# Rewriting the first attention of a gated two-branch layer, forward and backward, as two sweeps over head pairs

## The chip, the cores and the metric

The kernel runs on one core of one Trainium2 chip. The metric is the device time of one execution in microseconds; three runs of the kernel before gave a median of 16272.24 us (16250.68 to 16278.3). The engines are named as in the profile: PE is TensorE (matmuls; PEld its weight loads), DVE is VectorE, ACT is ScalarE, POOL is GpSimd, and SP and POOL are the queues that issue DMAs here.

## What is computed

The layer mixes two attentions of the same input with a gate, and the kernel returns the output and the gradients of eleven inputs (`grad_out` is given). All arrays are bf16.

```python
x = A_x                                            # (1, 2048, 576)
g = sigmoid((x * gate_w).sum(-1, keepdims=True))
out = g * A(x) + (1 - g) * B(x)

def A(x):                                          # 32 heads of 18, one shared K and V
    q = (x @ wq).reshape(1, 2048, 32, 18).transpose(0, 2, 1, 3)
    k, v = x @ wk, x @ wv                          # (1, 2048, 18)
    p = softmax(einsum('bhqd,bkd->bhqk', q, k) * 18 ** -0.5)
    o = einsum('bhqk,bkd->bhqd', p, v)
    return o.transpose(0, 2, 1, 3).reshape(1, 2048, 576) @ wo

def B(x):                                          # 64 segments of 32 tokens, 8 memory tokens
    mem = mem0
    for s in range(64):
        h = concatenate([mem, x[:, 32*s:32*s+32]])
        o = causal_attention(h, Wq, Wk, Wv) @ Wo   # 32 heads of 128
        mem, out_s = o[:, :8], o[:, 8:]
```

For the first attention the backward pass needs, per head, the probabilities P again, dP = dO V^T, dS = P (dP - delta) with delta the row sum of P dP, and from these dV = P^T dO, dK = dS^T Q and dQ = dS K.

## The kernel before

`build_full` calls the stages one after the other; a Tile framework draws the dependencies, orders the instructions of each engine ahead of time from a model of their costs, and places the waits. A tile with `bufs=n` has n buffers; one that is allocated again waits until the old contents have been used. [...]

Setup: `build_xT` (L161) transposes x, `load_A_weights` (L786) spreads the heads' 18 columns to 32, four heads to 128 columns, and `a_setup` (L813) makes K and V replicated on the four 32-row groups with a row of ones (`kaug`, `vaugT`), Q with a row that holds minus a bound of the scores (`qaugT`), and Q by token.

Forward sweep, `a_forward_attn` (L907): for each of 8 groups of four heads and 4 blocks of 512 queries, 16 iterations over 128 keys. Eight matmuls (L927; four row tiles of the array, each in two pieces of 256 columns) give the scores of four heads, two exponentials of 1024 columns (L932) the numerators, twelve matmuls in column tiles (L938; pieces of 171) the products with V and ones, and DVE adds them to an accumulator in SBUF (L940). At a block's end a matmul spreads the denominators and DVE inverts and normalizes. `a_forward_out` (L951) projects.

B follows: `b_forward` (L235), `make_transposed_weights` (L206), then `gate_combine_pass` (L655), which computes the gate, B's output projection from the stored oT, the output, dz, and the products da = g grad_out and db = (1-g) grad_out with db's transpose; `b_backward` (L414) and `b_epilogue` (L555).

Backward sweep, `a_backward` (L976): for each group of four heads it makes dO scaled by the denominators with a row for delta (`doaug`) and its form by token (`dotok`); then for each of 4 blocks of 512 keys and 16 tiles of 128 queries, one iteration: the scores again (L1067), four exponentials of 512 (L1072), dP (L1077), four products on DVE (L1082), dK by twelve matmuls (L1087) added to an SBUF accumulator by DVE (L1090), sixteen transposes of dS (L1095) and their copy to SBUF (L1097), dV (L1101, L1103), and dQ by sixteen matmuls and an addition (L1108, L1110). The four score tiles and the four dP tiles of an iteration share four PSUM banks (`b_sdA`). `a_final` (L1147) makes dx, dwq, dwk, dwv and dwo per tile of 128 tokens and adds the weight gradients in SBUF on DVE.

All matmuls go through `mm` (L97), transposes often through `tr` (L101), so L98 and L103 stand for many places; `evac` (L87) copies out of PSUM and alternates DVE (L93) and ACT (L95) by a counter. `pieces` (L42) cuts a matmul so that rows x columns x depth stay under 960000.

## Time and profile before

The profiled execution spans 16242.6 us, 29.6 us less than the median of the runs. Stages, cut by the first and last instruction of each (us from the span's start):

| stage | from, to | us |
|---|---|---|
| setup | 0, 167 | 167 |
| forward sweep of the first attention | 167, 1274 | 1107 |
| its output projection, B's weights loaded | 1274, 1388 | 114 |
| B forward | 1388, 6612 | 5224 |
| B's weights transposed | 6612, 6711 | 99 |
| gate and combine | 6711, 7075 | 364 |
| loads, B backward | 7075, 10122 | 3047 |
| B's weight gradients | 10122, 10985 | 863 |
| loads, transposes for the backward sweep | 10985, 11049 | 64 |
| backward sweep of the first attention | 11049, 15926 | 4877 |
| final pass | 15926, 16243 | 317 |

PE is busy 89% of the span, DVE 37%, ACT 26%, POOL 8%. A row of the groups gives line, engine, operation, out <- in, shapes and count, then busy us and mean ns of one, then the engine's idle time before them and what ended it. A shape K*M before the matmul's operand says how many rows and columns of the 128 x 128 array it uses. PEclk is the share of the full TensorE clock that was granted; a matmul's recorded time holds its latency too, so matmuls that follow each other overlap in the records. The timeline merges like instructions: start, length, engine, line, count.

### The profile page before, as it was taken

The page shows a single profiled execution, that of the slowest core. Times are in us where ns is not written, and L with a number is a line of the kernel's source. Part 1 is how long each engine was busy: PE and PEld are TensorE (multiplying, and loading weights), DVE is VectorE, ACT ScalarE, POOL GpSimd, SP SyncE. Part 2 cuts the span into 40 slices and gives each one's busy share as a digit, 9 for nine tenths or more (in the row PEclk, how much of TensorE's full clock was granted, in tenths as well). Part 3 has the DMA queues.
Part 4 walks back from the last instruction along what each step waited for, and adds up shares of the span by engine and source line. Part 5 has one row for each costly group of instructions (what it writes and reads, how often), then busy time and mean ns, then how long its engine had stood idle before and what let it go on. Part 6 is the DMA issues. An engine that isn't in the chain of part 4 may idle for free. (4 is left out here: it accounts for less than half of the span.)

```text
span 16242.6 us, 424152 instructions
## 1 busy us (share of the span) xinstructions
PE 14387.9 (89%) x194891; PEld 8837.7 (54%) x195001; DVE 6081.6 (37%) x8905; ACT 4154.2 (26%) x6200; POOL 1271.0 (8%) x2288
## 2 busy tenths in 40 slices
PE   8997999999999999769999999977898898898897
PEld 3334666666666666558888887333333333333333
DVE  3442333333333333323333333004454454454457
ACT  6882111111111111112222222002333333333330
POOL 0000000000000000111111111241000000000001
PEclk6555555555555555677777777995555555555556
DMA  1002111111111111442222223431000000000001
GB/s 44 9 9 97 37 39 39 39 39 39 39 39 39 38 38 39 144 138 83 85 80 82 83 85 97 135 105 47 13 1 13 13 1 13 13 1 13 7 1 50
DMA packets 473535, 780.13 MB, mean 48 GB/s; under 512 B 223841, under 2 KB 316818, under 8 KB 468866
## 3 DMA queue, kind: packets, MB, share of 16 engines
q1 hardware_dynamic: 357506, 429.32, 8.3%
q0 software_dynamic: 114240, 323.67, 5.8%
q8 instruction: 1524, 24.97, 0.6%
q14 instruction: 265, 2.17, 0.0%
HBM read 407.54 MB, written 345.18 MB: 46 GB/s over the span
## 5 line engine op out<-in xcount | busy, mean ns | idle before, releaser
L98 PEld LDWEIGHTS <-hTs 128*64 128x64 bf16 (+1 forms) x38400 | 1854.8, 150 | 951.9 <-DVE hTs L250 64.9
L1072 ACT ACTIVATE b_pexp<-b_sdA 128x512 bf16<-128x512 f32 x2048 | 1059.3, 609 | 1704.1 <-PE b_dkvp L98 1698.7
L1082 DVE TENSOR_TENSOR b_dsn<-b_sdA,b_pexp 128x512 bf16<-128x512 f32 x2048 | 1296.0, 684 | 290.9 <-PE b_sdA L98 288.9
L103 PE MATMUL b_ptrs<-identB,b_dsn 128*128 128x128 bf16 x8192 | 1245.8, 308 | 0.0
L98 PE MATMUL b_sdA<-b_kaug,b_qaug 19*128 19x256 bf16 x4096 | 1161.7, 401 | 5.4 <-ACT b_dotok L95 5.4
L98 PE MATMUL b_sdA<-b_vaugT,b_doaug 19*128 19x256 bf16 x4096 | 923.2, 395 | 179.2 <-ACT b_pexp L1072 178.3
L309 DVE RECIPROCAL rden<-pbank 64x512 f32<-64x512 f32 x256 | 840.5, 3322 | 482.6 <-PE pbank L98 482.6
L932 ACT ACTIVATE a_pexp<-a_sps 128x1024 bf16<-128x1024 f32 x1024 | 951.9, 1080 | 135.6 <-PE a_sps L98 128.9
L1090 DVE TENSOR_TENSOR b_dKTp<-b_dKTp,b_dkvp 128x512 f32<-128x512 f32 x512 | 351.8, 687 | 1563.7 <-PE b_dkvp L98 1563.7
L98 PE MATMUL pbank<-Wv,hTs 128*64 128x103 bf16 (+3 forms) x12800 | 912.4, 290 | 0.0
L103 PEld LDWEIGHTS <-b_dsn 128*128 128x128 bf16 x8192 | 705.5, 131 | 374.9 <-issue 374.9
L95 ACT COPY b_dsT<-b_ptrs 128x2048 bf16<-128x2048 bf16 x256 | 477.4, 1865 | 1458.5 <-PE b_ptrs L103 1458.5
L98 PE MATMUL b_dkvp<-b_dsn,b_qtokp 128*32 128x171 bf16 (+1 forms) x6144 | 813.7, 335 | 0.0
L98 PE MATMUL pbank<-Wq,hTs 128*64 128x103 bf16 (+1 forms) x10240 | 710.8, 290 | 85.7 <-DVE hTs L250 64.8
L98 PE MATMUL pbank<-Wqk,hTs 64*64 64x102 bf16 (+1 forms) x5120 | 752.8, 291 | 0.0
L98 PEld LDWEIGHTS <-b_qtokp 128*32 128x32 bf16 x6144 | 295.1, 110 | 786.2 <-issue 786.2
L98 PE MATMUL pbank<-Wk,hTs 128*64 128x103 bf16 (+1 forms) x10240 | 711.0, 290 | 0.0
L98 PE MATMUL pbank<-WoT,gTs 128*64 128x103 bf16 (+3 forms) x12800 | 644.6, 227 | 51.6 <-DMA WoT<-st_WoT 51.3
L98 PEld LDWEIGHTS <-b_doaug 19*128 19x128 bf16 x4096 | 220.5, 101 | 704.6 <-issue 704.4
L98 PE MATMUL a_sps<-a_qaugT,a_kaug 19*128 19x256 bf16 x4096 | 585.3, 402 | 1.1 <-ACT a_qtokp L95 1.1
L98 PEld LDWEIGHTS <-gTs 128*64 128x64 bf16 (+1 forms) x12800 | 458.8, 113 | 232.0 <-issue 52.4
L940 DVE TENSOR_TENSOR a_oacc<-a_oacc,a_pv 128x512 f32<-128x512 f32 x512 | 350.9, 685 | 565.0 <-PE a_pv L98 565.0
(409 smaller groups left out, 19900.9 us busy)
## 6 DMA issues: line engine op xcount, KB each, us to landing
st_q<-q SPq DMA_DIRECT2D x64, 512.0 KB
st_k<-k POOLq DMA_DIRECT2D x64, 512.0 KB, 3.0
st_vT<-vT SPq DMA_DIRECT2D x64, 512.0 KB
st_pnT<-pnT SPq DMA_DIRECT2D x64, 512.0 KB
st_oT<-oT POOLq DMA_DIRECT2D x64, 512.0 KB, 4.1
bq<-st_q SPq DMA_DIRECT2D x64, 512.0 KB
bvT<-st_vT SPq DMA_DIRECT2D x64, 512.0 KB
bk<-st_k POOLq DMA_DIRECT2D x64, 512.0 KB, 4.3
```

The lines of the kernel that those rows point to most:

```text
L95: nc.scalar.copy(out, in_)
L98: return self.nc.tensor.matmul(out, lhsT, rhs, start=start, stop=stop, tile_position=tp, skip_group_check=True)
L103: return self.nc.tensor.transpose(out, in_, self.identB[b:b + nrows, b:b + nrows], tile_position=tp)
L309: nc.vector.reciprocal(rden[rows, :], den[rows, :])
L932: nc.scalar.activation(pexp[:], spss[pr][:], ACT.Exp, scale=SCALEA)
L940: nc.vector.tensor_tensor(out=oacc[:, :], in0=oacc[:, :], in1=pv[:, :], op=ALU.add)
L1072: nc.scalar.activation(pe[:, :], sN[i][:, :], ACT.Exp, scale=SCALEA)
L1082: nc.vector.tensor_tensor(out=d_[:, :], in0=dps[i][:, :], in1=pexp[i][:, :], op=ALU.mult)
L1090: nc.vector.tensor_tensor(out=dKTp[:, k0:k0 + 512], in0=dKTp[:, k0:k0 + 512], in1=dkvp[:, :], op=ALU.add)
```

## The change

The first attention is rewritten around pairs of heads; each pair fills the four row groups of the array: two heads' Q and two heads' dO (rows 0, 32, 64, 96), against K, K, V, V.

- `prep` replaces `build_xT` and the gate's part of the combine pass: it loads x and grad_out whole, computes the gate, transposes x, da and db, and stores them. `combine_pass` keeps B's output projection, the output and dz; its pdg sums stay in PSUM.
- `a_weights`, `a_setup`: K and V in one tile `KV` (128 x 2048), and per key tile the stationary operands `VK` (V, a one, K) and `WK` (a one and K for the dP sums).
- `a_qd`: per pair and block of 512 queries, Q and dO in one tile `QD`, two column tiles at a time, with the score bound on Q; stored for the second sweep.
- `a_pass1` replaces the forward sweep. Per key tile: scores S of two heads, dP of two heads, E = exp(S), W = dP E, and four matmuls that add VK^T E and WK^T W into one PSUM bank over all 16 key tiles: sums of E, E V, E K, W and W K. `a_post` turns them at the block's end into O, delta and dQ = scale (WK - delta EK) / l, by token, mostly on POOL, and stores the scaled Q and dO (`SD`).
- `a_pass2` replaces the backward sweep's dK and dV. Delta has been put into two rows of the stored QD, so that dP comes out as dP - delta. Per block of 512 keys, over all 16 pairs and 16 query tiles: S, dP, E, dS = dP E, and four matmuls into one bank (dK of two heads, dV of two heads), copied out once per block.
- `a_out` projects O; `a_final` works on whole tensors kept in SBUF and adds the weight gradients in PSUM.

Matmuls of the first attention are no longer cut by `pieces`. The order of the stages is now prep, a_weights, a_setup, a_pass1, a_pass2, a_out, B forward, transposed weights, combine_pass, B backward, epilogue, a_final. The calls of `evac` without a named engine ahead of B forward go from 104 to 133, and the combine pass has none left (one per tile before).

The core of the diff (removed: `a_forward_attn` and `a_backward`, shown above):

```diff
+    def a_qd(self, p, qb, sp, psum):
...
+        pq = psum.tile([P, 512], F32, name="a_S", bufs=3)
+        for kt in range(NKT):
+            rows = KT_ROWS[kt]
+            self.mm(pq[0:64, :], lhsT=self.wqp[0:rows, kt, p, :], rhs=self.xT[0:rows, kt, q0:q0 + 512],
+                    start=(kt == 0), stop=False, tp=(0, 0))
+            self.mm(pq[64:128, :], lhsT=self.woTp[0:rows, kt, p, :], rhs=self.daT[0:rows, kt, q0:q0 + 512],
+                    start=(kt == 0), stop=(kt == NKT - 1), tp=(0, 64))
+        absq = sp.tile([64, 512], BF16, name="a_absq", bufs=2)
+        nc.scalar.activation(absq[:, :], pq[0:64, :], ACT.Abs)
+        self.mm(pq[0:64, :], lhsT=self.smneg[:, :], rhs=absq[:, :], start=False, stop=True, tp=(0, 0))
+        QD = sp.tile([P, 512], BF16, name="a_QD", bufs=3)
+        nc.scalar.copy(QD[:, :], pq[:, :])
+        (nc.sync if qb % 2 == 0 else nc.gpsimd).dma_start(self.qd_dram[p][:, q0:q0 + 512], QD[:, :])
+        return QD
+
+    def a_pass1(self, keep, sp, psum):
...
+        for p in range(NPR):
+            for qb in range(T // 512):
+                QD = self.a_qd(p, qb, sp, psum)
+                acc = psum.tile([P, 512], F32, name="a_acc", bufs=1)
+                for kt in range(NTT):
+                    k0 = kt * P
+                    S = [psum.tile([P, 512], F32, name="a_S", bufs=3) for _ in range(2)]
+                    dP = psum.tile([P, 2, 512], F32, name="a_dP", bufs=2)
+                    for i in range(4):
+                        r = slice(32 * i, 32 * i + 32)
+                        dst = S[i][:, :] if i < 2 else dP[:, i - 2, :]
+                        self.mm(dst, lhsT=self.KV[r, k0:k0 + P], rhs=QD[r, :], tp=(32 * i, 0))
+                    Et = sp.tile([P, 2, 512], BF16, name="a_E", bufs=3)
+                    Wt = sp.tile([P, 2, 512], BF16, name="a_W", bufs=3)
+                    for i in range(2):
+                        nc.scalar.activation(Et[:, i, :], S[i][:, :], ACT.Exp, scale=SCALEA)
+                    nc.vector.tensor_tensor(out=Wt[:], in0=dP[:], in1=Et[:], op=ALU.mult)
+                    for i in range(2):
+                        self.mm(acc[64 * i:64 * i + 64, :], lhsT=self.VK[:, kt, :], rhs=Et[:, i, :],
+                                start=(kt == 0), stop=False, tp=(0, 64 * i))
+                    for i in range(2):
+                        self.mm(acc[64 * i:64 * i + 64, :], lhsT=self.WK[:, kt, :], rhs=Wt[:, i, :],
+                                start=False, stop=(kt == NTT - 1), tp=(0, 64 * i))
+                self.a_post(p, qb, acc, QD, sp, psum, dl_all, dq_all, ot_all)
...
+    def a_post(self, p, qb, acc, QD, sp, psum, dl_all, dq_all, ot_all):
...
+        nc.scalar.copy(acs[:, :], acc[:, :])
+        pt = psum.tile([P, 4, P], F32, name="a_S", bufs=3)
+        for j in range(4):
+            nc.tensor.transpose(pt[:, j, :], acs[:, j * P:(j + 1) * P], self.identF[:])
...
+        nc.scalar.copy(tk[:].rearrange("p a b c -> p (a b c)"), pt[:].rearrange("p a b -> p (a b)"))
+        pd = psum.tile([P, 4, P], BF16, name="a_S", bufs=3)
+        for j in range(4):
+            self.tr(pd[:, j, :], QD[:, j * P:(j + 1) * P], P)
...
+        nc.scalar.copy(qt[:].rearrange("p a b c -> p (a b c)"), pd[:].rearrange("p a b -> p (a b)"))
...
+        nc.vector.reciprocal(rl[:, :, 1, :], tk[:, :, :, 18])
...
+        nc.gpsimd.tensor_tensor(out=SD[:], in0=qt[:],
+                                in1=rl[:].rearrange("p a b c -> p a (b c)").unsqueeze(3).to_broadcast([P, 4, 4, 32]),
+                                op=ALU.mult)
+        nc.gpsimd.dma_start(self.sd_dram[p][:, tts, :], SD[:].rearrange("p a b c -> p a (b c)"))
+
+    def a_pass2(self, keep, sp, psum):
...
+        for kb in range(T // 512):
+            k0 = kb * 512
+            acc = psum.tile([P, 512], F32, name="b_acc", bufs=1)
+            for p in range(NPR):
+                QD = sp.tile([P, T], BF16, name="b_QD", bufs=2)
+                nc.sync.dma_start(QD[:], self.qd_dram[p])
+                SD = sp.tile([P, NTT, P], BF16, name="b_SD", bufs=2)
+                nc.sync.dma_start(SD[:], self.sd_dram[p])
+                for qt in range(NTT):
...
+                    for i in range(4):
+                        r = slice(32 * i, 32 * i + 32)
+                        dst = S[i][:, :] if i < 2 else dP[:, i - 2, :]
+                        self.mm(dst, lhsT=QD[r, q0:q0 + P], rhs=KV[r, k0:k0 + 512], tp=(32 * i, 0))
...
+                    for i in range(2):
+                        nc.scalar.activation(Et[:, i, :], S[i][:, :], ACT.Exp, scale=SCALEA)
+                    nc.vector.tensor_tensor(out=dS[:], in0=dP[:], in1=Et[:], op=ALU.mult)
...
+                    for i in (2, 3, 0, 1):
+                        mv = dS[:, i, :] if i < 2 else Et[:, i - 2, :]
+                        self.mm(acc[32 * i:32 * i + 32, :], lhsT=SD[:, qt, 32 * i:32 * i + 32], rhs=mv,
+                                start=first, stop=last, tp=(0, 32 * i))
```

In `a_pass2` the tiles S (`b_S`), dP (`b_dP`), Et (`b_E`) and dS (`b_dS`) have the same shapes and numbers of buffers as S, dP, Et and Wt in `a_pass1`.

## Prediction, made before the change was built

> **What bounds the kernel now.** I read the page first, then the windows cut at the stage borders, then the timeline inside the two sweeps of the first attention, because the change lies there.

> ```profile
> span 16242.6 us, 424152 instructions
> core 0: us, PE busy (x) PEld busy (x) DVE busy (x) ACT busy (x) POOL busy (x), PEclk, DMA share, GB/s
> 0.00:167.00 167.00, 130.78 (x650) 50.12 (x661) 49.27 (x114) 50.21 (x87) 35.02 (x77) 0.97 0.28 97
> 167.00:1274.00 1107.00, 1002.83 (x10304) 344.53 (x10304) 474.30 (x575) 964.57 (x1056) 22.62 (x43) 0.50 0.03 10
> 1274.00:1388.00 114.00, 42.39 (x378) 24.38 (x385) 14.21 (x20) 16.71 (x17) 23.55 (x33) 0.66 0.69 256
> 1388.00:6612.00 5224.00, 4771.13 (x66114) 3449.23 (x66114) 1621.93 (x1662) 737.88 (x1280) 262.72 (x382) 0.50 0.11 38
> 6711.00:7075.00 364.00, 197.02 (x8302) 173.10 (x8301) 81.24 (x257) 16.95 (x39) 40.52 (x77) 0.74 0.46 152
> 10985.00:11049.00 64.00, 19.64 (x120) 11.53 (x121) 17.13 (x79) 4.24 (x8) 35.38 (x57) 0.50 0.69 197
> 11049.00:15926.00 4877.00, 4383.06 (x37304) 1866.78 (x37312) 2447.03 (x3938) 1546.70 (x2345) 99.09 (x123) 0.51 0.03 8
> 15926.00:16243.00 317.00, 228.67 (x1107) 90.42 (x1121) 242.67 (x427) 8.68 (x9) 38.84 (x57) 0.66 0.20 62
> ```

> The stages are, in order: setup, forward sweep, its output projection with the loading of B's weights, B's forward, combine, the loads of the first attention's backward, its backward sweep, the final pass. The two sweeps (1107 + 4877 = 5984 us) are what the change rewrites; both run at half the TensorE clock. Their inner loops, forward first:

> ```profile
> 598.93 7.82 ACT L932 ACTIVATE a_pexp<-a_sps 128x1024 bf16<-128x1024 f32 x8
> 601.03 0.60 PE L98 MATMUL a_sps<-a_qaugT,a_kaug 19*128 19x256 bf16 x4
> 601.14 0.69 DVE L940 TENSOR_TENSOR a_oacc<-a_oacc,a_pv 128x512 f32<-128x512 f32 x1 [1.19 <-PE a_pv L98]
> 601.57 0.33 PE L98 MATMUL a_pv<-a_pexp,a_vaugtok 128*32 128x171 bf16 x2
> 603.02 0.69 DVE L940 TENSOR_TENSOR a_oacc<-a_oacc,a_pv 128x512 f32<-128x512 f32 x1 [1.19 <-PE a_pv L98]
> ```
> ```profile
> 13000.14 0.62 PE L98 MATMUL b_dkvp<-b_pexp,b_dotok 128*32 128x171 bf16 x12
> 13001.47 2.07 ACT L1072 ACTIVATE b_pexp<-b_sdA 128x512 bf16<-128x512 f32 x4
> 13002.17 2.04 PE L98 MATMUL b_sdA<-b_vaugT,b_doaug 19*128 19x256 bf16 x8
> 13002.89 2.48 DVE L1082 TENSOR_TENSOR b_dsn<-b_sdA,b_pexp 128x512 bf16<-128x512 f32 x4 [0.31 <-PE b_sdA L98]
> ```

> Forward: one iteration (four heads, 128 keys, 512 queries) takes 603.02 - 601.14 = 1.88 us, which is two exponentials: ScalarE bounds it. 512 iterations make 963 us; the other 144 us are 32 block ends, 4.5 us each. Backward: 4877 / 512 = 9.5 us for the same work; PE is busy 90% of it, DVE 50%, ACT 32%. PE bounds it, and its largest item beside the scores is the transposes that the change removes:

> ```profile
> L1082 DVE TENSOR_TENSOR b_dsn<-b_sdA,b_pexp 128x512 bf16<-128x512 f32 x2048 | 1296.0, 684 | 290.9 <-PE b_sdA L98 288.9 <-ACT b_pexp L1072 1.8
> L103 PE MATMUL b_ptrs<-identB,b_dsn 128*128 128x128 bf16 x8192 | 1245.8, 308 | 0.0
> L1072 ACT ACTIVATE b_pexp<-b_sdA 128x512 bf16<-128x512 f32 x2048 | 1059.3, 609 | 1704.1 <-PE b_dkvp L98 1698.7 <-PE b_sdA L98 5.3
> ```

> **Prices.** Rows for a 512-column matmul, a 1024-wide DVE pass, and eight row tiles at once:

> ```profile
> L98 PE MATMUL a_pqt<-a_wqp,xT x154: 373/379/634, 49.5 to 165.6; 128*128 128x512 bf16 x122, 64*128 64x512 bf16 x32
> L93 DVE CAST a_qtokp<-a_pqt x8: 1224/1224/1225, 52.9 to 162.1; 128x1024 bf16<-128x1024 f32 x8
> ```
> ```profile
> 11065.17 0.62 PE L98 MATMUL b_sdA<-b_kaug,b_qaug 19*128 19x256 bf16 x8 [0.67 <-ACT b_dotok L95]
> ```

> A 512-column matmul records 379 ns at full clock and 634 at half; the 255 ns between are about what 512 columns take once more, so I take 0.21 us of columns at full clock, 0.43 at half (0.83 ns a column), and the rest (0.17 to 0.20) as latency that a stream hides. Eight row tiles of 256 columns take 0.62 us, that is two rounds of 0.21 and latency: four row tiles run together. Twelve column tiles of 171 columns take 0.62: three rounds, four together. From a row-tiled group to a column-tiled one, 601.57 - 601.03 = 0.54 us pass for two rounds (0.43): a change of tiling costs 0.11. Four DVE products in 2.48 us, the last lasting 0.684, start 0.60 apart; 1224 - 684 = 0.54 for 512 more, so the 1024-wide product costs 1.14. Four exponentials in 2.07 us start 0.49 apart.

> [...]

> **The change, part by part.** *Pass 1* has 64 blocks (16 pairs, 4 query blocks) of 16 iterations. Each has four row-tiled matmuls of 512 (one round, 0.43 at half clock), two exponentials (0.98), one DVE product (1.14) and four matmuls of 64 columns' width, two together (two rounds, 0.85). PE at half clock: 0.43 + 0.85 + two changes of tiling = 1.50. Does the clock rise? These rows bracket it:

> ```profile
> 1283.96 3.19 PE L98 MATMUL a_pa<-a_wop,a_ontall 128*128 128x512 bf16 x7
> 1284.60:1288.00 3.40, 3.40 (x14) 1.63 (x13) 0.00 (x0) 0.00 (x0) 0.00 (x0) 0.50 0.35 134
> 1288.00:1291.40 3.40, 3.00 (x37) 1.79 (x37) 1.42 (x2) 1.93 (x2) 1.04 (x2) 1.00 0.27 94
> 4027.98 14.26 PE L98 MATMUL pbank<-Wv,hTs 128*64 128x103 bf16 x200
> ```

> Count how much of the array streams. Seven full matmuls of 512 in 3.19 us fill it (7 x 0.43 = 2.99, 94%) and the next window has full clock. B's projection, 200 half-wide matmuls of 103 columns in 14.26 us, fills 200 x 0.5 x 103 x 0.83 ns / 14.26 us = 60%, and B's forward stays at 0.50. The forward sweep's eight quarter-high tiles of 256 and twelve quarter-wide ones of 171 are 1024 full columns, 0.85 of 1.88 us (45%), and it stays at 0.50. Pass 1 would fill 1.28 of 1.50, 85%; if the two buffers of dP held it back (product done, 0.85 and 0.43 of columns, a change, 0.20 latency, 0.1 for two semaphores: 1.69 us) still 76%. I take it that the clock rises; then columns halve, that loop is about 1.0, and DVE's 1.14 bounds. ACT is close behind: 16 x 0.98 and five operations at a block's end (the absolute value, the copy of QD, of the sums, of two transposed tiles) at 0.49 make 18.1 us to DVE's 18.2. At that end a new wait stands on ACT: its copy of the sums waits for the last W matmul, the next block's exponentials are queued behind it, and DVE and PE wait for those; the projection of the next QD takes a bank of a_S meanwhile. I price a block's end like the forward sweep's, 4.5 us, the nearest row; between 0 (three buffers of E cover it) and 8. Pass 1: 64 x (16 x 1.14 + 4.5) = 1455.

> *Pass 2*: 1024 iterations, the same but its sums are four tiles of 32 together, one round. PE at half clock 0.43 + 0.43 + 0.22 = 1.08; the dP loop 0.43 + 0.11 + 0.43 + 0.20 + 0.1 = 1.27; fill 0.85 / 1.27 = 67%, nearer to the 60% that stayed slow. I take half clock and 1.27: 1024 x 1.27 + 4 x 4.5 = 1318 (at full clock 1185). Its loads, 1 MB in 20 us, hide behind that: the combine stage moved 152 GB/s. Between the passes a transpose of the row sums, 32 small DMAs and a reload: 25 us.

> Two sweeps: 1455 + 25 + 1318 = 2798 instead of 5984: -3186.

> *Other stages.* The backward's 64 us of loads and transposes go; what it needs is made in prep. The final pass loads five tensors of 2.4 MB (47 us at the 256 GB/s of the third window), does 16 tiles of about 3 us and accumulates its weight gradients in PSUM instead of DVE (400 matmuls, about 55 us): 160 for 317, -157, bounds 120 to 280. Setup loses the 154 query matmuls above and its own projections move into pass 1; prep adds 160 transposes and 64 evictions on DVE and ACT, about 40 us, part beside the loads: 100 for 167, -67, bounds 80 to 180. Output projection: 114 kept, plus or minus 20. Combine:

> ```profile
> 6726.43 1.58 SPq L681 DMA_DIRECT2D c_oT<-st_oT  x2
> 6736.53 6.59 PE L98 MATMUL c_pb<-WoN,c_oT 128*32 128x171 bf16 x278 [1.24 <-DMA c_oT<-st_oT]
> 6749.26 1.25 SPq L681 DMA_DIRECT2D c_oT<-st_oT  x2
> ```

> A tile takes 22.8 us, 10 of them waiting for four loads of oT; dropping the stores of b, da, db and dbT (0.75 of 3.1 MB) frees about 2 us a tile: -32, between 0 and -60. One thing moves that the diff does not show: evac alternates DVE and ACT by a counter. Before B it was called 104 times, now 133, so in B every pair swaps engines:

> ```profile
> L95 ACT COPY qT<-ptrh 128x1024 bf16<-128x1024 bf16 x64 | 64.8, 1012 | 65.1 <-PE ptrh L103 65.1
> L93 DVE COPY qT<-ptrh 128x1024 bf16<-128x1024 bf16 x64 | 44.2, 691 | 244.1 <-PE ptrh L103 244.1
> ```

> 0.32 us a copy, some three a segment on the path, 64 segments, two sweeps: between -120 and +120; I take 0.

> POOL's new work, about ten small operations a block, stays beside:

> ```profile
> L1044 POOL TENSOR_TENSOR b_prod<-b_dopT,b_ont 128x512 bf16<-128x512 bf16 x32 | 37.0, 1156 | 41.2 <-DVE b_dopT L1042 36.8 <-DMA b_daTs<-daT_dram 4.1
> ```

> A 512-wide product takes 1.16 us; one of that size and nine of at most 144 make under 8 us of a 23 us block. The stores of SD queue behind them on POOL, those of QD on SP and POOL by turns, and nobody waits for either before pass 2.

> Sum: -3186 - 64 - 157 - 67 - 32 = -3506, so 16243 becomes 12737. The median of the runs, 16272, is 30 above the span: 12767, say 12770.

> **Rivals.** *Full clock in both passes* (chance 0.17): pass 2 1185, block ends half hidden (64 x 2.2 less): 12770 - 133 - 144 = 12490. [...] The trace speaks against busy time as the measure: the forward sweep is 91% busy at 0.50 for 1107 us.

> *Half clock throughout* (0.25). S has three banks for two heads, and block-end tiles share them. If the row tiles are issued in two groups, pass 1 is 2 x 0.43 + 0.85 + 4 x 0.11 = 2.15 us (fill 60%, so it stays slow), pass 2 1.72: 64 x 38.9 + 1024 x 1.72 + 43 = 4294, hence 12770 + 1496 = 14270. For it: in the backward, eight row tiles waiting for slots took 2.04 us instead of 0.62.

> *Slower than before* (0.05): the static order alternates single row and column tiles, nothing overlaps, half clock: 8 x 0.43 + 8 x 0.11 = 4.3 us in both passes, 64 x 73.3 + 1024 x 4.3 + 43 = 9137, hence 19100. It decides from a mean of 2.9 us per iteration of both passes. Against it: four tiles together in both forms above.

> *The stash does not hide* (0.04): pass 2 waits for its 1 MB per pair, 5 us at the pace of the combine's four loads (2 MB in 10 us): 64 x 5 = +320 if none overlapped, 13090. Against it: both tiles have two buffers.

> **How the numbers follow.** The forecast (0.49, own range 12600 to 13100) gives 12770. From 12400 (below the first rival, with DVE's floor nearly reached) to 14270 all but the slower case and the tail above is held, about 0.85. About 0.2% is what a measurement here tells from no change: faster 0.94, same 0.01, slower 0.05.

> **What would show it.** Right: clock near 1.0 in pass 1, DVE products back to back at 1.14 there, block ends of 4 to 5 us, pass 2 at 0.5 with 1.27, b stages unchanged within 2%. Wrong: 0.50 in pass 1; row tiles starting in more than one group; DVE waiting for b_QD loads; pass 2 at 1.14 with full clock (forecast too high).

## The result and the profile after

The changed kernel takes 13516.99 us (median of 4 runs, 13495.15 to 13530.5) against 16272.83 before: a ratio of 0.831 (95% interval 0.830 to 0.832), 2756 us less. The forecast was 12770 in a range of 12400 to 14270: the direction held and the time lies in the range, but the gain was put 750 us too high. The profiled execution spans 13528.8 us, 792 more than the 12737 that the prediction summed to. The windows of the changed kernel, cut at the stage borders:

```profile
span 13528.8 us, 358100 instructions
core 0: us, PE busy (x) PEld busy (x) DVE busy (x) ACT busy (x) POOL busy (x), PEclk, DMA share, GB/s
0.00:117.00 117.00, 62.18 (x392) 33.32 (x392) 51.64 (x134) 19.73 (x50) 36.87 (x88) 1.00 0.43 144
117.00:2128.00 2011.00, 1464.89 (x9390) 457.97 (x9389) 1264.33 (x1087) 1295.04 (x2364) 289.76 (x788) 0.85 0.03 10
2128.00:2160.00 32.00, 3.97 (x30) 2.96 (x28) 1.15 (x2) 3.67 (x7) 14.38 (x31) 0.50 0.57 189
2160.00:3602.00 1442.00, 1418.72 (x8192) 254.00 (x8192) 1235.86 (x1026) 1112.94 (x2052) 11.24 (x13) 0.51 0.18 56
3602.00:3648.00 46.00, 36.36 (x244) 16.48 (x245) 10.34 (x24) 11.85 (x24) 8.17 (x15) 0.89 0.38 118
3648.00:8900.00 5252.00, 4758.01 (x66107) 3437.53 (x66106) 1648.19 (x1659) 743.78 (x1277) 264.37 (x384) 0.50 0.11 39
...
9398.00:12520.00 3122.00, 2898.16 (x66367) 2504.54 (x66367) 1040.67 (x1662) 711.68 (x1215) 316.24 (x700) 0.75 0.27 78
12520.00:13399.00 879.00, 743.72 (x3685) 311.65 (x3682) 54.01 (x78) 45.41 (x78) 335.48 (x635) 0.97 0.41 124
13399.00:13529.00 130.00, 87.95 (x718) 45.53 (x718) 22.18 (x44) 14.88 (x29) 43.69 (x58) 0.83 0.41 131
```

Beside the forecast (for B's stages: their time before):

| stage | forecast | measured | difference |
|---|---|---|---|
| setup | 100 | 117 | +17 |
| pass 1 | 1455 | 2011 | +556 |
| between the passes | 25 | 32 | +7 |
| pass 2 | 1318 | 1442 | +124 |
| output projection | 114 | 46 | -68 |
| B forward | 5224 | 5252 | +28 |
| B's weights transposed, combine, loads | 482 | 498 | +16 |
| B backward | 2996 | 3122 | +126 |
| B's weight gradients | 863 | 879 | +16 |
| final pass | 160 | 130 | -30 |

The differences sum to 792. Four of them matter: pass 1, pass 2, B backward, and the output projection on the other side. B backward does the same work as before, with its alternating copies on the other engine; its row in the trace of before shows a little more clock:

```profile
7126.00:10122.00 2996.00, 2788.52 (x66368) 2456.05 (x66368) 1040.82 (x1664) 720.22 (x1216) 329.38 (x719) 0.77 0.26 83
```

**Pass 1.** The clock rose as forecast (0.85), but DVE, which was to bound the pass, is busy for 1264 of 2011 us. From the starts of the 1024 products: 960 steps inside a block take 1.52 us in the mean (666 of them lie wholly at full clock and take 1.44, 207 wholly at half clock, 1.73), and the 63 steps over a block's end take 8.66. What DVE waits for, in the view of the tile a_W:

```profile
L892 DVE TENSOR_TENSOR a_W<-a_dP,a_E x1024: 1212/1224/1226, 119.7 to 2126.4; 128x1024 bf16<-128x1024 f32 x171
its engine sat idle before it (us, times) until:
  ACT a_E L891: 480.3, 790
```

The timeline of two steps at full clock (cut at `...`) shows why:

```profile
1012.86 1.22 DVE L892 TENSOR_TENSOR a_W<-a_dP,a_E 128x1024 bf16<-128x1024 f32 x1 [0.26 <-ACT a_E L891]
...
1014.13 0.41 PE L99 MATMUL a_acc<-a_W,a_WK 128*64 128x512 bf16 x2 [0.54 <-DVE a_W L892]
...
1014.26 1.22 DVE L892 TENSOR_TENSOR a_W<-a_dP,a_E 128x1024 bf16<-128x1024 f32 x1 [0.18 <-ACT a_E L891]
1014.35 0.41 PE L99 MATMUL a_acc<-a_E,a_VK 128*64 128x512 bf16 x2
...
1014.69 0.39 PE L99 MATMUL a_S<-a_QD,a_KV 32*128 32x512 bf16 x1
1014.69 0.39 PE L99 MATMUL a_dP<-a_QD,a_KV 32*128 32x512 bf16 x2
1014.70 0.38 PE L99 MATMUL a_S<-a_QD,a_KV 32*128 32x512 bf16 x1
...
1015.11 1.09 ACT L891 ACTIVATE a_E<-a_S 128x512 bf16<-128x512 f32 x2 [0.40 <-PE a_S L99]
...
1015.74 1.22 DVE L892 TENSOR_TENSOR a_W<-a_dP,a_E 128x1024 bf16<-128x1024 f32 x1 [0.26 <-ACT a_E L891]
```

Follow it as a chain. The product of step n (1012.86; that of step n+1 starts at 1014.26) ends at 1014.08 (1012.86 + 1.22). Only then can PE issue the W matmuls of step n (1014.13). Behind them in PE's queue stand the E matmuls of step n+1 and then a score matmul of step n+2 (1014.69). Its exponential runs from 1015.11 to 1015.71, and the product of step n+2 starts at 1015.74. From product n to product n+2 that is 2.88 us, 1.44 a step. DVE, ACT and PE each have time to spare; the order on PE strings them together.

A block's end is a chain too. Its instructions in the timeline, at half clock:

```profile
1027.27 1.22 DVE L892 TENSOR_TENSOR a_W<-a_dP,a_E 128x1024 bf16<-128x1024 f32 x1 [0.26 <-ACT a_E L891]
...
1029.23 0.59 ACT L916 COPY a_acs<-a_acc 128x512 f32<-128x512 f32 x1 [1.99 <-PE a_acc L99]
1029.87 1.12 PE L919 MATMUL a_S<-identF,a_acs 128*128 128x128 f32 x4 [0.68 <-ACT a_acs L916]
1031.08 0.58 ACT L921 COPY a_tk<-a_S 128x512 f32<-128x512 f32 x1 [1.26 <-PE a_S L919]
1031.34 0.64 PE L99 MATMUL a_S<-xT,a_wqp 128*64 128x512 bf16 x1
...
1033.87 0.59 ACT L863 ACTIVATE a_absq<-a_S 64x512 bf16<-64x512 f32 x1 [1.72 <-PE a_S L99]
1035.12 0.58 ACT L866 CAST a_QD<-a_S 128x512 bf16<-128x512 f32 x1 [0.67 <-PE a_S L99]
...
1037.49 1.23 DVE L892 TENSOR_TENSOR a_W<-a_dP,a_E 128x1024 bf16<-128x1024 f32 x1 [5.53 <-ACT a_E L891]
```

The sums are copied, transposed and copied again; the projections of the next QD stand behind that on PE, then the absolute value, the bound, the copy of QD, and only then the next scores: 10.2 us from product to product here.

**Pass 2** rises to full clock after two steps, falls to half at a wait for a load, and stays there:

```profile
2161.60:2165.00 3.40, 3.40 (x16) 0.46 (x14) 2.27 (x2) 1.61 (x4) 3.36 (x4) 0.50 0.96 376
2165.00:2199.00 34.00, 22.24 (x229) 7.99 (x224) 33.08 (x30) 31.55 (x59) 6.28 (x7) 1.00 1.02 362
2199.00:2207.00 8.00, 2.99 (x17) 0.64 (x18) 1.24 (x2) 1.85 (x4) 0.00 (x0) 0.51 1.06 120
2207.00:3602.00 1395.00, 1389.17 (x7931) 244.70 (x7930) 1199.08 (x993) 1076.88 (x1985) 0.00 (x0) 0.50 0.15 47
```

30 products in 34 us at full clock are 1.13 us a step, DVE back to back; at half clock a step takes 1.41. The wait is for the third pair's b_QD, whose buffer came free while 12 MB of B's weights were on the queues (362 GB/s in the second row).

### The profile page after: what moved, and what is told of

Same layout as the page of the kernel before. It is cut to its first block, busy times and chain, and to the rows that moved or that the text cites. A ratio compares the mean times of both kernels' runs of the same rounds, so it can differ in the third digit from the quotient of the medians.

```text
span 13528.8 us, 358100 instructions
## 1 busy us (share of the span) xinstructions
PE 11751.1 (87%) x163974; PEld 7294.4 (54%) x163974; DVE 5404.0 (40%) x5901; ACT 4011.9 (30%) x7182; POOL 1399.6 (10%) x2859
## 5 line engine op out<-in xcount | busy, mean ns | idle before, releaser
L892 DVE TENSOR_TENSOR a_W<-a_dP,a_E 128x1024 bf16<-128x1024 f32 x1024 | 1251.5, 1224 | 572.8 <-ACT a_E L891 480.3
L979 DVE TENSOR_TENSOR b_dS<-b_dP,b_E 128x1024 bf16<-128x1024 f32 x1024 | 1235.6, 1223 | 204.6 <-PE b_S L99 153.9
L891 ACT ACTIVATE a_E<-a_S 128x512 bf16<-128x512 f32 x2048 | 1115.9, 596 | 447.2 <-PE a_S L99 388.1
L978 ACT ACTIVATE b_E<-b_S 128x512 bf16<-128x512 f32 x2048 | 1110.9, 595 | 349.1 <-DVE b_dS L979 183.2
L99 PE MATMUL b_S<-b_KV,b_QD 32*128 32x512 bf16 x2048 | 888.1, 583 | 32.0 <-DMA b_QD<-qd_dram 31.9
L99 PE MATMUL b_acc<-b_dS,b_SD 128*32 128x512 bf16 x2048 | 619.6, 601 | 12.2 <-DVE b_dS L979 10.2
L99 PE MATMUL b_acc<-b_E,b_SD 128*32 128x512 bf16 x2048 | 620.3, 602 | 3.1 <-DMA b_SD<-sd_dram 2.1
L99 PE MATMUL b_dP<-b_KV,b_QD 32*128 32x512 bf16 x2048 | 615.1, 597 | 0.0
L99 PE MATMUL a_S<-a_QD,a_KV 32*128 32x512 bf16 x2048 | 539.4, 441 | 45.6 <-ACT a_QD L866 43.1
L99 PE MATMUL pkq<-maskbias,identB 64*64 64x64 bf16 x2048 | 532.5, 260 | 0.0
```

Source lines behind the costliest of these rows:

```text
L99: return self.nc.tensor.matmul(out, lhsT, rhs, start=start, stop=stop, tile_position=tp, skip_group_check=True)
L891: nc.scalar.activation(Et[:, i, :], S[i][:, :], ACT.Exp, scale=SCALEA)
L892: nc.vector.tensor_tensor(out=Wt[:], in0=dP[:], in1=Et[:], op=ALU.mult)
L978: nc.scalar.activation(Et[:, i, :], S[i][:, :], ACT.Exp, scale=SCALEA)
L979: nc.vector.tensor_tensor(out=dS[:], in0=dP[:], in1=Et[:], op=ALU.mult)
```

## The experiments

Each kernel is the changed kernel with the edit shown or named. The four runs of the changed kernel spread over 35 us, so single runs are read by the stage that the edit touches.

**The counter of evac.**

```diff
+                    k._evac_i += 1
                     k.b_forward(bw, bsp, bps, wo_pool=bwo)
```

> The changed kernel with one more count of the evac counter ahead of B forward, so that B's alternating copies go to the engines they had before. Theory (the swap costs B time): B backward, 3122 us in the changed kernel and 2996 before, comes back to about 2996, B forward (5252 and 5224) to about 5224; total about 13517 - 150 = 13365. Rival (the swap is worth nothing; B backward lost time to something else, since its clock is 0.75 instead of 0.77): B backward stays at 3110 to 3130, total 13500 to 13530.

It took 13349.29 us. B forward and B backward:

```profile
3640.00:8853.00 5213.00, 4762.05 (x65943) 3441.36 (x65942) 1621.86 (x1659) 738.82 (x1277) 263.90 (x383) 0.50 0.12 39
9349.00:12351.00 3002.00, 2793.71 (x66368) 2457.02 (x66368) 1041.65 (x1664) 720.95 (x1216) 319.27 (x703) 0.77 0.28 82
```

B backward is back at 3002, with its clock of 0.77, and B forward at 5213: 120 + 39 = 159 us less in the two stages (168 by the totals, one run against a median). So much did a counter cost that no line of the diff sets.

**A third buffer for pass 2's loads**: `bufs=2` to `bufs=3` for `b_QD` and `b_SD`.

> The changed kernel with three buffers instead of two for b_QD and b_SD. Theory (pass 2 starts at full clock with 1.13 us an iteration and is thrown to half clock by one load wait of 10 us at 2195 us, from which it doesn't return): pass 2 stays at full clock, 1024 x 1.131 + 20 = about 1180 us instead of 1442; total about 13260, up to 30 more where part of B's weights now comes after pass 2. Rival (its loop falls to half clock by itself within the first pairs, or at the next block of keys): pass 2 about 1430, clock 0.5 to 0.6, total about 13510.

It took 13539.86 us. The load wait is gone, and the theory fell all the same:

```profile
2187.00:2276.00 89.00, 70.37 (x629) 22.41 (x626) 88.71 (x79) 84.94 (x159) 0.00 (x0) 1.00 0.16 51
2276.00:3605.00 1329.00, 1328.38 (x7535) 228.12 (x7532) 1131.61 (x943) 1023.18 (x1886) 0.00 (x0) 0.50 0.14 46
```

Full clock lasted 89 us instead of 34, over a stretch in which DVE never waited, and then went without a load to blame. So the wait only sets when the clock falls. In this kernel B's weights are loaded only after pass 2 (from 3614 us on), presumably because the third buffers take their memory, and the output projection goes from 46 to 74 us.

**Another order of issue in pass 1, and its control.** In e3_scores_ahead the code names dP of step n, the scores of step n+1, the product, and the sums of step n-2:

```diff
+                scores(0)
                 for kt in range(NTT):
+                    dP = ...                       # two matmuls
+                    if kt + 1 < NTT:
+                        scores(kt + 1)             # two matmuls, two exponentials
                     nc.vector.tensor_tensor(out=Wt[:], in0=dP[:], in1=Et[:], op=ALU.mult)
+                    held.append((kt, Et, Wt))
+                    while len(held) > 2 or (kt == NTT - 1 and held):
+                        k_, E_, W_ = held.pop(0)   # its four sums
```

> The changed kernel with another order of issue in pass 1: dP of key tile n with the scores of tile n+1, and the sums of tile n-2 behind them (five buffers of E for it). Theory (one iteration of pass 1 is half of a chain over two: product 1.22, W matmuls 0.05 and E matmuls 0.56 on PE, scores 0.42, exponential 0.60, that is 2.88 / 2 = 1.44, because PE has the scores queued behind W matmuls that wait for DVE): the chain is cut, iterations inside a block go from a mean of 1.52 to 1.15 to 1.2 us, pass 1 from 2011 to about 1660 to 1710 with block ends as they are (8.7 us); total about 13170 to 13220. Rival (the two dP buffers, or ACT and DVE together, set the pace): iterations stay at 1.40 to 1.50 at full clock, total 13470 to 13530.

e9_five_e has the five buffers of E without the new order:

> The changed kernel with five buffers of E in pass 1 and nothing else, the control of e3_scores_ahead, which had both five buffers and the new order of issue. Theory (the order on PE is what binds): iterations inside a block stay at 1.44 us at full clock, pass 1 1990 to 2040. Rival (the buffers of E held the exponentials back): 1.13 to 1.2, pass 1 about 1660.

e3_scores_ahead took 13171.12 us, e9_five_e 13502.97. Pass 1 of the first:

```profile
115.00:1752.00 1637.00, 1358.85 (x9392) 413.92 (x9389) 1194.16 (x1087) 1256.06 (x2365) 290.55 (x788) 0.90 0.03 12
```

and of the second:

```profile
117.00:2125.00 2008.00, 1461.56 (x9390) 455.56 (x9389) 1264.67 (x1087) 1295.40 (x2365) 290.59 (x788) 0.85 0.03 10
```

With the order changed the steps at full clock take 1.13 us (673 of them, from the starts of the products), which is DVE back to back; with the buffers alone they stay at 1.44. The order on PE was the bound.

**The end of a block.** e4_qd_early makes the next block's QD at the ninth key tile:

```diff
+                    if kt == 8:
+                        QD_next = self.a_qd(...)   # of the next block
```

> The changed kernel with the QD of the next block made at the ninth key tile of this block instead of behind its end. Theory (a block's end is a chain: copy of the sums, transposes, their two copies, projections of the next QD, absolute value, bound, copy, scores; 8.7 us from product to product instead of 1.5, some 4.5 of them from the projections on): ends fall to about 4 us, 63 x 4.5 = 285 less, and the clock drops less often, 30 to 60 less; pass 1 about 1670 to 1730 us. Rival (the projection's bank is one of the three of the scores; held in the middle of a block it stops the iterations for as long as the end took): pass 1 1950 to 2050.

e6_pair_qd makes the four QDs of a pair together, with eight buffers:

```diff
+            QDs = [self.a_qd(p, qb, sp, psum) for qb in range(T // 512)]
             for qb in range(T // 512):
-                QD = self.a_qd(p, qb, sp, psum)
+                QD = QDs[qb]
```

> The changed kernel with the QD of a pair's four blocks made together at the pair's start (eight buffers). Theory (the projection of the next QD is 4.5 us of the 8.7 us at a block's end): 48 of 63 ends fall to about 4.2 us, the 15 at a new pair rise to about 12; pass 1 2011 - 48 x 4.5 + 15 x 3.5 = about 1850 us, a little less if the clock drops less often. Rival (the ends are set by the chain through the sums, transposes and copies of the block that ends): ends of 8 us inside a pair, pass 1 2000 or more.

They took 13405.03 and 13382.6 us. Pass 1 of e4_qd_early, then of e6_pair_qd:

```profile
117.00:1999.00 1882.00, 1631.29 (x9390) 483.61 (x9389) 1243.64 (x1087) 1266.32 (x2364) 292.90 (x788) 0.88 0.03 11
```
```profile
115.00:1981.00 1866.00, 1453.10 (x9386) 463.19 (x9384) 1257.38 (x1087) 1283.98 (x2364) 292.01 (x788) 0.90 0.03 11
```

In e4_qd_early the ends fall from 8.66 to 5.2 us, 217 less in all, but the steps inside a block rise from 1.52 to 1.61, 88 more; the step in which the QD is made takes 4.0 us instead of 1.4. The rival's mechanism is real and takes back two fifths, so that pass 1 falls by 129 us where 280 to 340 were expected. In e6_pair_qd the ends inside a pair are 5.3 us, those at a new pair 12.6. So of 8.7 us some 3.4 belong to the QD of the next block; the other 3.7 above a plain step belong to the sums of the block that ends.

**Does the clock follow the fill?** Three kernels give pass 2 the order of e3_scores_ahead and one more matmul a step, with zeros as its stationary operand, into the sum bank. They differ in its columns: 512, 8 and 128.

```diff
+                        self.mm(acc[:, 0:N], lhsT=self.zero[:, :], rhs=E_[:, 0, 0:N], start=False, stop=False)
```

> The changed kernel with pass 2 issued as dP of step n, scores of step n+1, sums of step n-2, and one more matmul an iteration: a stationary operand of zeros (128 x 128) against 512 columns of E, added to the sum bank, so that nothing changes in the sums. Theory (the clock follows how much of the array is fed; pass 2 falls to half clock because it feeds 61% there, and it can't get out; more fill lifts it out, and at full clock PE still has less than DVE's 1.13 us to do): clock near 1.0 over pass 2, 1.13 us an iteration, pass 2 about 1180 us instead of 1442, total about 13260 although work is added. Rival (the extra matmul doesn't lift the clock, and PE is the bound at half clock with three rounds of 0.43 and tiling changes): 1.6 to 1.7 us an iteration, pass 2 1640 to 1740, total about 13770.

> The same as e5_fill2 with the extra matmul cut from 512 columns to 8: the same places of issue, hardly any fill. Theory (fill decides): clock about 0.5 in most of pass 2, 1.3 to 1.45 us an iteration, pass 2 1330 to 1490 us. Rival (the new order of issue, not the fill, gives what e5_fill2 gives): pass 2 about 1180 at full clock here too.

> e5_tiny2 with the extra matmul at 128 columns: between the 8 columns that stayed at half clock (0.85 us of full columns in 1.30 us, 66%) and the 512 that rose. 0.96 in about 1.33 us is 72%. Theory (the border for rising lies near 67 to 69%, as the stages of the kernel before bracket it): the clock rises, pass 2 about 1190 to 1220 us, total about 13280. Rival (the border is higher, or only bank-wide work counts): pass 2 1340 to 1400 at half clock, total about 13360 to 13400.

They took 13300.27, 13345.87 and 13258.67 us. Pass 2 with 512, with 8 and with 128 columns:

```profile
2176.00:3380.00 1204.00, 1087.29 (x9212) 394.66 (x9212) 1162.52 (x1026) 1112.40 (x2052) 12.53 (x15) 0.98 0.21 68
```
```profile
2152.00:3494.00 1342.00, 1318.12 (x9212) 383.19 (x9212) 1248.72 (x1026) 1113.19 (x2052) 12.13 (x14) 0.50 0.19 61
```
```profile
2153.00:3350.00 1197.00, 1167.63 (x9212) 392.47 (x9212) 1164.03 (x1026) 1112.56 (x2052) 12.24 (x15) 0.97 0.21 69
```

The new order of issue (with four buffers of E and two of dS) gives 1342 instead of 1442 us at half clock (1.30 us a step). Added work that computes nothing gives another 140, because it lifts the clock (PEclk 0.98 and 0.97 for 0.50): 128 columns are enough, and 512 cost no more. In the tiny case the two useful rounds, 0.85 us of full columns in 1.30, fill 65% and the clock stays down; with 128 columns (0.11 more, in about the same time) it is 73% and rises. So these runs put the border of this loop between 65 and 73%; the 67 to 69% in the expectation of e8_fill128 were the author's estimate from stages of the kernel before. The extra matmul adds to the share of the array and to the time in which columns stream alike, so these runs don't tell which of the two counts. Fill alone doesn't tell it either: in the changed kernel's row 2161.60:2165.00 above, behind which its pass 2 rose, 15 matmuls start, each on a quarter of the array, which is 15 x 0.25 x 0.43 = 1.6 us of full columns in 3.4, 47%, less than in the loop that stayed slow (0.85 in 1.41, 60%).

**All together**: pass 1 as one stream over all blocks in the new order, QD by pair, a_post split so that the copy of the sums stays at the end and the rest stands at the fifth key tile of the next block; pass 2 as e5_fill2; the counter as e1_parity.

> All together: pass 1 as one stream over blocks with the order of e3_scores_ahead, QD by pair, the rest of a block's end (transposes, copies, POOL's part) put at the fifth key tile of the next block; pass 2 as e5_fill2; the counter as e1_parity. Theory: pass 1 1024 x 1.131 + 16 x 6 + 64 x 1 = about 1320 us instead of 2011, pass 2 1180 instead of 1442, B 168 less: 13517 - 690 - 260 - 168 = about 12400. Rival (a block's end in the midst of the next one stops the stream for as long as before, through the banks of a_S): pass 1 1600 to 1700, total 12700 to 12800.

It took 12501.36 us (12487.25 to 12510.81, 4 runs), a ratio of 0.769 to the kernel before (0.767 to 0.770). Pass 1, pass 2, B forward and B backward:

```profile
115.00:1480.00 1365.00, 1213.85 (x9385) 382.47 (x9384) 1183.94 (x1087) 1237.27 (x2364) 291.55 (x788) 1.00 0.04 15
1509.00:2709.00 1200.00, 1086.40 (x9212) 394.79 (x9212) 1161.42 (x1026) 1112.40 (x2052) 12.13 (x14) 0.98 0.21 68
2755.00:7970.00 5215.00, 4763.77 (x66011) 3443.61 (x66008) 1621.50 (x1659) 738.14 (x1277) 263.81 (x383) 0.50 0.12 39
8470.00:11498.00 3028.00, 2813.99 (x66368) 2473.68 (x66368) 1041.66 (x1664) 720.28 (x1216) 317.73 (x703) 0.76 0.27 81
```

Pass 1 holds full clock throughout. 48 of its block ends now cost no more than a step, the 15 at a new pair 8.9 us each; the steps inside a block, which hold the rest of a_post, take 1.22 us in the mean. Pass 1 is 45 us over its forecast, pass 2 20, B backward 32.

**A dense stretch in B forward.** B forward is the largest stage and runs at half clock. The last two kernels add to e7_all nine, then eight matmuls of zeros once a segment, when the first bank of its projections is complete; the extra matmul of pass 2 has 128 columns here.

```diff
+                    if which == 'q' and u == 0:
+                        for _ in range(9):
+                            self.mm(pb[:, :], lhsT=self.zero[:, :], rhs=self.w_nat('q', 0)[0][0:P, 0:512],
+                                    start=False, stop=False)
```

> e7_all with the extra matmul of pass 2 at 128 columns as in e8_fill128, and nine matmuls of 512 columns with a stationary operand of zeros in B forward, once a segment, into the first bank of its projections when that is complete: 3.8 us at half clock that add nothing to the result. Theory (a stage keeps full clock on less fill than it needs to rise, so that a short dense stretch is enough): B's projections (600 half-wide matmuls of 103 columns a segment) go from 1.42 us per 20 matmuls at half clock to 0.93, both as measured where B ran at either clock; 580 / 20 x 0.49 = 14.2 us saved and 3.8 spent per segment, 64 x 10.4 = 665, total 12500 - 665 = about 11835. Rival (the clock falls back as soon as the dense stretch ends, or the stretch is too short to raise it): 64 x 3.8 = 245 added, total about 12745.

> [...]

e10_kick took 11852.91 us (11839.66 to 11862.32), ratio 0.729 (0.728 to 0.731); e11_kick8 11798.33 (11763.85 to 11831.62), ratio 0.726 (0.723 to 0.728). The timeline of e10_kick around one stretch, then the windows of B forward in e10_kick and in e11_kick8:

```profile
3466.63 0.55 PE L99 MATMUL pbank<-Wq,hTs 128*64 128x102 bf16 x8
...
3467.34 4.02 PE L99 MATMUL pbank<-Wq,zero 128*128 128x512 bf16 x9
3471.29 0.56 PE L99 MATMUL pbank<-Wq,hTs 128*64 128x103 bf16 x8
...
3471.99 0.38 PE L99 MATMUL pbank<-Wq,hTs 128*64 128x103 bf16 x8
```
```profile
2755.00:7290.00 4535.00, 4069.25 (x66068) 2923.78 (x66066) 1600.47 (x1643) 728.96 (x1264) 262.28 (x380) 0.69 0.13 45
```
```profile
2740.00:7230.00 4490.00, 3999.60 (x65689) 2895.29 (x65754) 1601.46 (x1646) 730.06 (x1267) 264.93 (x385) 0.70 0.13 45
```

Within a microsecond of the stretch the same eight matmuls take 0.38 us instead of 0.55, and B forward goes from 5215 us to 4535 and 4490. In e11_kick8 full clock comes in all 64 segments, at the latest 2 us after the stretch, and lasts 27 to 31 us (the PEclk of 0.70 over its 4490 us is 28 us of full clock a segment). Its time had been expected at that of e10_kick, 11820 to 11870 us. The two kernels change part of the computation, though, against what the expectation of e10_kick says: both return the gradient of B's Wk, which comes from dS^T Q, wrong by 0.447 of its size. Each piece of the bank begins with `start`, the stretch behind them has none, and the number fits a bank in which four of the five pieces were left at zero: with Q at zero in a fifth of its columns (four fifths of one bank in four) a fifth of that gradient's squares would be missing, and the root of 0.2 is 0.447. That is an estimate from this one number; a trace holds no values, and no run shows how the pieces came to be zero. The stretch adds matmuls and changes no other instruction, so the time is read here for the clock alone; these are not kernels to use, and a stretch ahead of the pieces, with a `start` of its own, wasn't tried. The zeros of pass 2 change no gradient in e7_all. The kernel to use is e7_all.

## Why the prediction was right in direction and too high in size

That the time lies in the range is luck: the range reached up to 14270 for a rival that didn't come, and the forecast's own range, 12600 to 13100, missed 13517.

- **The prices held.** The 1024-wide product was priced at 1.14 us from start to start; where nothing else binds it takes 1.13 (30 products in the 34 us of pass 2 at full clock). The 0.43 and 0.21 us taken for 512 columns are in the trace of before: the seven matmuls from 1283.96 to 1286.53 start 0.43 apart at half clock, and 512-column matmuls of B's weight gradients 0.22 apart at full clock. The four row tiles start within 0.01 us of each other (1014.69 to 1014.70 above) and last 0.38 to 0.39, as one matmul of 512 columns does (0.38 at full clock): they cost one round, so the rival of 14270, with row tiles in two groups, did not come.
- **"Columns halve, that loop is about 1.0, and DVE's 1.14 bounds"** is the step that failed, 291 us of pass 1's 556 (960 x (1.443 - 1.14)). The sum had each engine's busy time and the loop through the two buffers of dP, but not the order on PE: scores of step n+2 stand behind the W matmuls of step n, which wait for DVE. e3_scores_ahead changes that order, with more buffers of E for it, and e9_five_e shows that it wasn't the buffers. The same loop is longer at half clock (1.73), and the clock falls at block ends: 76 us more, 960 x (1.522 - 1.443).
- **A block's end at 4.5 us** was mis-sized: 8.66 - 1.52 = 7.1 above a plain step. Beside the forecast that is 63 x (8.66 - 1.14 - 4.5) = 190 us. The sum named the wait on ACT but put the next QD's projection beside it ("meanwhile"); it runs behind it, since it stands behind the transposes on PE. e4_qd_early and e6_pair_qd put 3.4 us of it there.
- **Pass 2 at half clock** was right (the fill, taken as 67% and "nearer to the 60%", is 0.85 / 1.41 = 60%). The 60% itself was read too high: 40 of the 200 matmuls of B's projection have 64 rows, so it fills 54%. The mechanism held, only the 1.27 us was too low, 124 us in all. Its 0.1 for two semaphores can be read from the traces: 0.05 us pass from the end of a copy of b_dsT (13001.57 in the trace of before) to the matmul that it releases (13001.62), and as much from product to W matmul in the changed kernel (1014.08 to 1014.13). Scores issue late there: two score matmuls that take 0.61 together spread over 1.07 in its timeline, as the three banks come free one exponential at a time. That this is the cause is only argued; issuing the scores a step ahead (e5_tiny2) brings 1.30.
- **The counter "between -120 and +120; I take 0"**: the parity cost 154 us in this profile (28 + 126), and e1_parity gets 159 back in the same two stages. The mechanism was named, its bound was too tight: it counted copies only, and B backward also loses clock (0.75 for 0.77, and 0.77 again in e1_parity).
- **The output projection "kept"** was wrong by 68 us: the loads of B's weights, which filled that stage, moved beside pass 2. The windows show it (256 GB/s in that stage before, 362 in pass 2's first 34 us), and e2_three_stash, which sends them back, has 74 us there.
- **The stash rival** (chance 0.04) came once: a wait of 8 us. Setup, combine and the final pass lay within 30 us.
- **The full-clock rival** (chance 0.17) came in neither pass as a whole: pass 1 reached 0.85, and in pass 2 PE is busy in 1389 of 1395 us and stays at 0.50, more plainly than the forward sweep of before (91% busy at 0.50). So busy time alone doesn't raise the clock here. B forward, busy for 91% of its time in e7_all, stayed at 0.50 too; in e11_kick8 one stretch a segment of eight matmuls of 0.43 us was enough to raise it.

## What to carry to other kernels

Busy times and buffer loops aren't enough to bound a software pipeline: write down the order on the engine that feeds the others, and follow one item through it; a matmul that waits for the slowest engine must not stand ahead of what that engine needs two steps later (1.44 us a step here, 1.13 with the order changed). A stage that keeps TensorE busy at half clock may be short of fill and not of time (pass 2 took 1342 us at 65%, 1197 at 73%): measure columns times share of the array against what the time could take, and try a little dense work, in a bank where it can't change a sum, before cutting work. When a change adds calls of a helper that alternates engines, look at who gets which engine downstream.
